# Moving two passes of a weight conversion from VectorE to GpSimd, with the first group's feed-forward blocks made for 128 tokens

## The chip, the cores and the metric

The kernel runs on one core of a Trainium2 chip. The metric is the device time of one execution in microseconds, and it is given as the median over runs. The engines that matter here are TensorE (PE in the profile, with its weight loads as PEld), VectorE (DVE), ScalarE (ACT), GpSimd (POOL) and the queue of SyncE (SP) that issues most transfers.

## The reference: what is computed

Two blocks follow each other. The first is an mLSTM cell over q, k, v of shape (4, 8, 768, 40): batch 4, 8 heads, 768 positions, 40 values per head. The second is a feed-forward block over the 3072 tokens that come out, with 320 features each.

```python
# mLSTM, for each position t:
m_new = max(f + m, i);  C = exp(f + m - m_new) * C + exp(i - m_new) * outer(v, k);  n likewise with k
y[t] = sigmoid(o) * (C @ q) / max(abs(n . q), 1)
# bridge: (B, H, S, D) -> (B*S, H*D), 3072 x 320
a = x @ w1;  b = x @ w2          # 320 -> 1024
out = ((a * b) @ w3) @ w_out     # 1024 -> 1024 -> 320
```

The weights arrive as 64-bit floating-point numbers and are made into 32-bit ones on the chip. The feed-forward block folds w3 and w_out into one matrix of 1024 x 320 before it is used.

## The kernel before, in words

**Steps.** The 3072 tokens are cut into 24 units of 128 tokens (6 chunks of positions by 4 batches). The main loop (L568) runs over steps s; unit s is worked on in step s. A step's work on TensorE is, in this order: the transposes `pt` of k and q (`turn`, L281), the transposes `px` of an earlier unit's output y (`x_trans`, L388), a fold of weights `wp` if one is ready (`w3_mm`), output products `po` (`ffn_out`), up-projections `pa` and `pb` (`up`, L521), their remainder in four 64x64 quarters (`up_rest`, L534), and the cell's small matrix products into the one PSUM tile `cell` (`quarter_work`, L308). The order on TensorE is fixed by a chain of dependencies that `in_order` (L82) adds: each instruction waits in its place.

**Groups.** Four units are a group of 512 tokens, with one `xT` tile. `ups` (L554) lists the up-projections. Each entry is two blocks of 128 hidden features by 256 tokens, for all groups; in group 0 the blocks are ordered so that the first four blocks of features come for both halves of the tokens, then the other four. `n_up` says how many entries a step makes: none up to step 3, one in steps 4 and 5, two from step 6 on. In a step with one entry, `x_trans` of unit s - 2 is placed between `up` and `up_rest` (L595); other steps turn unit s - 3 at their start (L587).

**After the cell's products** VectorE multiplies the scores with the decay weights (`pw`, L346), updates the state (with a product `decayed` on GpSimd between), and makes y of unit s - 1 in `outputs` (L362 to L382). The next step's `cell` products need the same PSUM tile, so they wait for the last reading of it (L370). GpSimd then copies the last 64 features of y once more beside themselves (`twice`, L386), and `x_trans` reads that copy too. `twice(s - 2)` is called in step s ahead of the feed-forward work, on the y that step s - 1 made.

**GpSimd's other work** in a step: two masks of the next unit's weights (`weights`, L278), the weighted values `vw` (`weighted`, L300) and the product of the state with its decay (`decayed`, L305). In the kernel before, `weighted(s)` and, from step 4 on, the first `decayed` of unit s are called at the start of step s.

**Conversion.** `fetch` (L199) brings a piece of a weight as pairs of 32-bit words, `raw`; ScalarE scales the high words (`scale`, L173), and `to_f32` (L175) makes five VectorE passes over the piece: L184, L185 and L186 make the main part `ex` and the power `ma` from the high words, L187 multiplies the low words by that power, L188 adds both. The pieces are, in order, w1 and w2 (10 of 512 columns), w_out (8 of 320) and w3 (16 of 512, of which each is turned by a VectorE transpose, L237). `n_cvt` (L563) says how many pieces are converted at the end of a step: 2, 1, 1, 1, 2, 2, 3, 3, 3, then 2 in each of seven steps. Four rotating `raw` tiles let `fetch` run up to three pieces ahead, on SP's queue.

**Order.** Up to the end of step 6 (`pinned = 7`, L629) the order in which the program calls the instructions is kept on every engine (`keep_order`, L455). After that a planner with its own costs orders the engines other than TensorE.

Of the kernel before, what the change touches and what calls it, by code (L numbers as in the profile page):

```python
# [8 lines left out]
FP = mybir.dt.float32  # L9
U32 = mybir.dt.uint32  # L10
AF = mybir.ActivationFunctionType
OP = mybir.AluOpType
# [4 lines left out]
def kernel(  # L17
# [26 lines left out]
    nc = tc.nc  # L44

    B, H, S, D = q.shape
    L = 64
    P = 128
    NT = S // L
    NT2 = S // P  # L50
    NU = NT2 * B
# [6 lines left out]
    FO = DFF // P  # L58
    KF = DM // P
    REM = DM - KF * P  # L60
    GT = B
# [4 lines left out]
    wst = ctx.enter_context(tc.tile_pool(name="wst", bufs=2))  # L66
# [39 lines left out]
    state = [[const.tile([P, NP, D1], FP, name=f"state{b}_{i}") for i in range(3)] for b in range(B)]  # L106
# [13 lines left out]
    def load(n):  # L120
        for dst, src in ((kbuf[n % NB][:, :, 0:D], k), (qbuf[n % NBQ][:, :, 0:D], q), (vbuf[n % NB][:, :, 0:D], v)):
            if src is not q or n < N_DVE:
                nc.sync.dma_start(out=dst, in_=rows(src, n))
# [11 lines left out]
    def load_o(n):  # L135
        o_t[n] = io.tile([P, H, D], FP, name="o_in", tag="o_in", bufs=4)
        nc.sync.dma_start(out=o_t[n], in_=rows(o_gate, n))

    def load_u(n):
        c, b = divmod(n, B)  # L140
        src = U_d[2 * c:2 * c + 2, b * H:(b + 1) * H, :].rearrange("x h t -> x (h t)")
        for x in range(2):
            nc.sync.dma_start(out=weights_tile(n)[halves[x]].rearrange("p h t -> p (h t)"),
                              in_=src[x:x + 1].to_broadcast([L, H * L]))
# [12 lines left out]
    CW = 512  # L157
# [14 lines left out]
        hi = raw[:, :, 1].bitcast(FP)  # L172
        nc.scalar.mul(out=hi, in_=hi, mul=2.0 ** -111)  # L173

    def to_f32(dst, raw):  # L175

        n = dst.shape[-1]
        lo, hi = raw[:, :, 0], raw[:, :, 1]  # L180
        t = wst.tile([128, n], U32, name="ex", tag="ex", bufs=1)
        r = wst.tile([128, n], U32, name="ma", tag="ma", bufs=1)
        V = nc.vector
        V.tensor_scalar(out=t, in0=hi, scalar1=3, scalar2=None, op0=OP.logical_shift_left)  # L184
        V.scalar_tensor_tensor(out=t, in0=hi, scalar=0x80000000, in1=t, op0=OP.bitwise_and, op1=OP.bitwise_or)  # L185
        V.tensor_scalar(out=r, in0=t, scalar1=0xFF800000, scalar2=None, op0=OP.bitwise_and)  # L186
        V.scalar_tensor_tensor(out=r.bitcast(FP), in0=lo, scalar=2.0 ** -52, in1=r.bitcast(FP), op0=OP.mult, op1=OP.mult)  # L187
        V.tensor_tensor(out=dst, in0=t.bitcast(FP), in1=r.bitcast(FP), op=OP.add)  # L188

    def cols(c0, n):  # L190
# [28 lines left out]
    w3T_t = {}  # L219
    turned_w3, ready_w3 = [], []  # L220

    def scale_next():
        scaled.append(pend.pop(0))
        scale(scaled[-1][1])

    def convert():
        if not scaled:
            scale_next()
        dst, raw, ko, half = scaled.pop(0)
        if dst is not None:  # L230
            to_f32(dst, raw)
            return
        w3 = wst.tile([128, CW], FP, name="w3", tag="w3")
        to_f32(w3, raw)
        if half == 0:
            w3T_t[ko] = wst.tile([128, FO, 128], FP, name="w3T", tag="w3T")
        nc.vector.transpose(out=w3T_t[ko].rearrange("c k (m r) -> c m k r", r=32)[:, 2 * half:2 * half + 2],  # L237
                            in_=w3.rearrange("r (m k c) -> r m k c", m=2, k=FO))
        if half:
            turned_w3.append(ko)  # L240

    def fold():
# [15 lines left out]
    def out_gate(n):  # L258
        nc.scalar.activation(out=o_t[n], in_=o_t[n], func=AF.Tanh, scale=0.5)
# [11 lines left out]
    def weights(n):  # L271
        c, b = divmod(n, B)
        src = weights_tile(n) if c else spread(n)
        pw = weights_tile(n)
        for h in range(H):
            nc.scalar.activation(out=pw[:, h, :], in_=src[:, h, :], func=AF.Exp, bias=aT[:, c, b * H + h:b * H + h + 1])  # L276
        for r in halves:
            nc.gpsimd.affine_select(out=pw[r], in_=pw[r], compare_op=OP.is_ge, fill=0.0, base=0,  # L278
                                    pattern=[[0, H], [1, L]], channel_multiplier=-1)
# [17 lines left out]
    def weighted(n):  # L297
        c, b = divmod(n, B)
        vw_t[n] = sb.tile([P, H, D1], FP, name="vw", tag="vw")
        nc.gpsimd.tensor_tensor(out=vw_t[n], in0=vbuf[n % NB], op=OP.mult,  # L300
                                in1=wT[:, c, b * H:(b + 1) * H].unsqueeze(2).to_broadcast([P, H, D1]))

    def decayed(new, old, n, x):
        c, b = divmod(n, B)
        nc.gpsimd.tensor_tensor(out=new, in0=old, op=OP.mult, in1=decay[:, b * NP:(b + 1) * NP, 2 * c + x:2 * c + x + 1]  # L305
                                .to_broadcast([P, NP, D1]))
# [78 lines left out]
    def twice(n):  # L385
        nc.gpsimd.tensor_copy(out=y_t[n][:, DM:DM + REM], in_=y_t[n][:, KF * P:DM])  # L386

    def x_trans(n):  # L388
        gr, j = divmod(n, GT)
        if j == 0:  # L390
            x_t[gr] = ffn.tile([128, KF + 1, TG], FP, name="xT", tag="xT")
        y = y_t.pop(n)
        px = mps([128, KF + 1, P], "px")
        for cc in range(KF + 1):
            transpose(px[:, cc, :], y[:, cc * P:(cc + 1) * P])
        nc.scalar.copy(out=x_t[gr][:, :, j * P:(j + 1) * P], in_=px)  # L396
# [7 lines left out]
    gates = const.tile([P, 2 * TB], FP, name="gates")  # L404
# [61 lines left out]
    V = nc.vector  # L466
# [7 lines left out]
    for i, r in enumerate(third):  # L474
        V.tensor_tensor_scan(out=M[r, 1:GC + 1], data0=F3[r, :, L - 1], data1=U3[r, :, L - 1], initial=M[r, 0:1],
                             op0=OP.add, op1=OP.max)
# [25 lines left out]
    for i, r in enumerate(third):  # L502
        nc.gpsimd.tensor_tensor(out=pick[r, :, i, :], in0=pair[r].to_broadcast([BH, B * NP, GC]), op=OP.mult,
                        in1=dec[r].unsqueeze(1).to_broadcast([BH, B * NP, GC]))
# [39 lines left out]
    def ffn_out(gr, j):  # L544
        po = mps([P, DM], "po")
        for f in range(FO):
# [4 lines left out]
        nc.scalar.dma_start(out=out[t0:t0 + P, :], in_=o_sb)  # L551


    ups = [(0, [f, f + 1], slice(j * 2 * P, (j + 1) * 2 * P)) for part in range(0, FO, FO // 2) for j in range(2)  # L554
           for f in range(part, part + FO // 2, 2)]
    ups += [(gr, [f, f + 1], slice(j * 2 * P, (j + 1) * 2 * P)) for gr in range(1, NG) for j in range(2)
            for f in range(0, FO, 2)]
    downs = [(gr, j) for gr in range(NG) for j in range(GT)]
    n_up = [0] * 4 + [1] * 2 + [2] * 23 + [0]
    n_down = [0] * 17 + [2] * 10 + [0, 0, 4]  # L560
    w12 = [("w12", i, part) for part in range(2) for i in range(2 * KF + 1)]
    todo = w12[KF * 2 + 1:] + [("wo", i, 0) for i in range(FO)] + [("w3", ko, part) for ko in range(FO) for part in range(2)]
    n_cvt = [2, 1, 1, 1, 2, 2, 3, 3, 3] + [2] * 7  # L563
    pinned = 7
    behind = ExitStack()
    turned, converted, fetched = 0, 2, 2 * KF + 1

    for s in range(len(n_up)):  # L568
        if B <= s + 3 < NU:
            load_u(s + 3)  # L570
        if s + 2 < NU:
            load(s + 2)
            load_o(s + 2)
        if 0 < s < B - 1:
            weights(s + 1)
            out_gate(s)
        if s < NU:
            weighted(s)
            if s >= B:
                decayed(state[s % B][1], state[s % B][0], s, 0)  # L580
            if 0 < s < N_DVE:
                turn(s)
        if 0 <= s - 2 < NU:
            twice(s - 2)
        if N_DVE <= s + 1 < NU:
            load_turned(s + 1)
        while turned < min(s - 2, NU):  # L587
            x_trans(turned)
            turned += 1
        fold()  # L590
        for _ in range(n_down[s]):
            ffn_out(*downs.pop(0))
        now = [ups.pop(0) for _ in range(n_up[s])]
        open_ups = [up(*x) for x in now]
        if len(now) == 1 and turned == s - 2 < NU:  # L595
            x_trans(turned)
            turned += 1

        def rest():
            for x in open_ups:  # L600
                up_rest(*x)

        gated = None
        if s <= NU:
            gated = quarter_work(s, rest)
        else:
            rest()
        with tc.issue_after(gated.ins) if gated else nullcontext():
            if N_DVE <= s + 1 < NU:
                turn(s + 1)  # L610
        if s == 0:
            gate_cols(g, gT, nc.scalar.copy)
            out_gate(0)
            scale_next()
            weights(1)
        if s == NU:
            cell_psum.close()
            banks.append(ctx.enter_context(tc.tile_pool(name="ps_x", bufs=4, space=bass.MemoryType.PSUM)))
        if B - 1 <= s < NU:
            if s + 1 < NU:  # L620
                weights(s + 1)
            out_gate(s)
        for _ in range(n_cvt[s] if s < len(n_cvt) else 0):
            convert()
            converted += 1
        while todo and fetched < converted + (2 if s < 2 else 3):
            fetch(*todo.pop(0))
            fetched += 1
        if s + 1 == pinned:  # L629
            for ins in keep_order(front):  # L630
                behind.enter_context(tc.issue_after(ins))
# [30 lines left out]
```

## Time and profile before

| | us |
|---|---|
| median of 3 runs (lowest, highest) | 483.41 (482.39, 483.81) |
| the profiled execution's own time | 483.81 |
| its span, first to last instruction | 482.1 |
| TensorE busy | 454.6 (94%) |
| VectorE busy | 259.9 (54%) |
| ScalarE busy | 146.8 (30%) |
| GpSimd busy | 86.6 (18%) |

The busy shares are averages over a start, in which VectorE is full and TensorE has gaps, and a long second part, in which TensorE has none. Steps are best told by their last product of the scores (`cell<-qT,kT`), which ends a step on TensorE: at 46.0 us for step 3, 56.5 for step 4, 66.2 for step 5, 78.6 for step 6, 92.7 for step 7 and 109.9 for step 8. From step 8 on TensorE's products follow each other closely to the end.

### The profile page before, as it was taken

To read this page: it belongs to the slowest core of one execution; us is meant where nothing else is said; L and a number is where in the kernel's file an instruction comes from. 1 tells how busy PE (TensorE), PEld (TensorE's weight loads), DVE (VectorE), ACT (ScalarE), POOL (GpSimd) and SP (SyncE) were. 2 spreads that over 40 slices of the span, in tenths; PEclk is the share of its full clock that TensorE was granted. 3 is DMA by queue.
4 is the path that set the end of the run, shared out by engine and by line. 5 is a ranking of instruction groups with operands and counts; after the bars stand their busy time and mean duration, and the time that the engine had idled before them with its cause. 6 is when DMAs were issued, how large, how long until landed. Compare 5 with 4: busy or idle time off the path is not lost.

```text
span 482.1 us, 12855 instructions
## 1 busy us (share of the span) xinstructions
PE 454.6 (94%) x5402; PEld 365.6 (76%) x5402; DVE 259.9 (54%) x526; ACT 146.8 (30%) x399; POOL 86.6 (18%) x165
## 2 busy tenths in 40 slices
PE   3868999799999999999999999999999998999997
PEld 2757877678878888788878787787877877778864
DVE  7797798989886968887451533614325033011110
ACT  3644545443442353354331321311101111011011
POOL 5442322520220322213220211201000000000000
PEclk9995999989999999999999999999999999999999
DMA  8999977599698656433350623324020000000001
GB/s 183 166 166 200 194 139 137 114 203 191 125 189 135 127 127 148 94 66 57 77 132 15 141 57 96 66 81 110 3 82 16 14 27 3 29 14 16 1 14 41
DMA packets 116185, 45.72 MB, mean 95 GB/s; under 512 B 96736, under 2 KB 107168, under 8 KB 116128
## 3 DMA queue, kind: packets, MB, share of 16 engines
q1 hardware_dynamic: 112528, 40.88, 43.4%
q10 hardware_dynamic: 3600, 4.03, 2.4%
q8 instruction: 42, 0.69, 0.6%
q14 instruction: 15, 0.12, 0.1%
HBM read 40.86 MB, written 4.03 MB: 93 GB/s over the span
## 4 chain that ended last, share of the span: by engine, by line
PE 81%; issue 7%; DVE 7%; POOL 2%; DMA 1%; ACT 1%; ACTq 0%; SPq 0%; POOLq 0%; DVEq 0%
PE pa L90 23%; PE po L90 22%; PE pb L90 16%; PE cell L90 9%; PE wp L90 7%; PE pt L93 2%; DVE h L370 1%; PE px L93 1%; PE ub L90 1%; POOL pw L278 1%; DVE o_in L380 1%; DVE h L366 1%; DMA raw<-in_moe_w_out_dram 1%; POOL state L305 1%; DMA gates<-in_i_gate_dram 1%
## 5 line engine op out<-in xcount | busy, mean ns | idle before, releaser
L542 DVE TENSOR_TENSOR ab<-pb,a_sb 128x512 f32<-128x512 f32 x48 | 33.0, 689 | 162.1 <-ACT a_sb L541 162.0
L90 PE MATMUL po<-w3o,ab 128*128 128x320 f32 x384 | 105.4, 433 | 1.3 <-DVE h L370 1.3
L90 PEld LDWEIGHTS po<-w3o,ab 128*128 128x128 f32 x384 | 72.2, 190 | 30.7 <-issue 1.5
L90 PE MATMUL pa<-xT,w 128*128 128x256 f32 x384 | 92.5, 384 | 0.9 <-ACT xT L396 0.6
L90 PE MATMUL pb<-xT,w 128*128 128x256 f32 x384 | 90.8, 379 | 0.0
L90 PEld LDWEIGHTS pa<-xT,w 128*128 128x128 f32 x384 | 73.3, 193 | 14.1 <-ACT xT L396 1.0
L90 PEld LDWEIGHTS pb<-xT,w 128*128 128x128 f32 x384 | 72.9, 190 | 10.3 <-DVE ab L542 0.4
L541 ACT ACTIVATE a_sb<-pa 128x512 f32<-128x512 f32 x48 | 28.6, 595 | 151.3 <-PE pb L90 151.3
L90 PE MATMUL pa<-xT,wr 64*64 64x256 f32 x384 | 47.0, 383 | 0.0
L90 PE MATMUL pb<-xT,wr 64*64 64x256 f32 x384 | 47.0, 383 | 0.0
L305 POOL TENSOR_TENSOR state<-state,decay 128x164 f32<-128x164 f32 x40 | 19.6, 495 | 146.9 <-PE cell L90 91.5
L278 POOL TENSOR_SCALAR_AFFINE_SELECT pw<-pw 64x512 f32<-64x512 f32 x48 | 35.5, 740 | 47.8 <-ACT pw L276 46.2
L276 ACT ACTIVATE pw<-pw,aT 128x64 f32<-128x64 f32 x160 | 40.7, 338 | 8.1 <-DMA pw<-U_d 8.1
L90 PEld LDWEIGHTS pa<-xT,wr 64*64 64x64 f32 x384 | 25.8, 133 | 16.8 <-issue 7.8
L90 PE MATMUL wp<-wo,w3T 128*128 128x320 f32 x128 | 35.9, 433 | 0.1
L90 PEld LDWEIGHTS cell<-vbuf,pw 64*64 64x64 f32 x768 | 27.5, 141 | 6.1 <-issue 1.9
L549 ACT COPY o_sb<-po 128x320 f32<-128x320 f32 x24 | 10.2, 423 | 67.9 <-PE po L90 63.6
L90 PEld LDWEIGHTS wp<-wo,w3T 128*128 128x128 f32 x128 | 23.7, 190 | 9.1 <-PE px L93 0.3
L90 PE MATMUL cell<-vbuf,pw 64*64 64x41 f32 x768 | 27.4, 231 | 2.2 <-issue 1.3
L386 POOL COPY y<-y 128x64 f32<-128x64 f32 x24 | 7.1, 296 | 108.1 <-DVE y L382 104.2
L90 PEld LDWEIGHTS pb<-xT,wr 64*64 64x64 f32 x384 | 25.8, 133 | 0.0
L346 DVE TENSOR_TENSOR pw<-cell,pw 128x512 f32<-128x512 f32 x24 | 16.4, 684 | 15.3 <-PE cell L90 15.2
(89 smaller groups left out, 514.0 us busy)
## 6 DMA issues: line engine op xcount, KB each, us to landing
raw<-in_moe_w_dram SPq DMA_DIRECT2D x64, 128.0 KB, 3.2
pw<-U_d SPq DMA_DIRECT2D x40, 128.0 KB, 3.6
kbuf<-in_k_dram SPq DMA_DIRECT2D x24, 160.0 KB, 4.4
vbuf<-in_v_dram SPq DMA_DIRECT2D x24, 160.0 KB, 5.0
o_in<-in_o_gate_dram SPq DMA_DIRECT2D x24, 160.0 KB, 4.0
out_dram<-o_sb ACTq DMA_DIRECT2D x24, 160.0 KB, 1.9
raw<-in_moe_w_dram SPq DMA_DIRECT2D x7, 512.0 KB, 5.9
qbuf<-in_q_dram SPq DMA_DIRECT2D x17, 160.0 KB, 4.8
```

What stands on the lines that cost most here:

```text
L90: in_order(nc.tensor.matmul(out, lhsT=lhsT, rhs=rhs, start=start, stop=stop))
L93: in_order(nc.tensor.transpose(out, in_, ident[0:n, 0:n]))
L276: nc.scalar.activation(out=pw[:, h, :], in_=src[:, h, :], func=AF.Exp, bias=aT[:, c, b * H + h:b * H + h + 1])
L278: nc.gpsimd.affine_select(out=pw[r], in_=pw[r], compare_op=OP.is_ge, fill=0.0, base=0, pattern=[[0, H], [1, L]], channel_multiplier=-1)
L305: nc.gpsimd.tensor_tensor(out=new, in0=old, op=OP.mult, in1=decay[:, b * NP:(b + 1) * NP, 2 * c + x:2 * c + x + 1] .to_broadcast([P, NP, D1]))
L346: first_read = nc.vector.tensor_tensor(out=pv, in0=ss, in1=pv, op=OP.mult)
L366: nc.vector.tensor_tensor(out=h.rearrange("p (n two) d -> p two n d", two=2), in0=pi, in1=gT[:, c, hs].rearrange("p (n two) -> p two n", t ...
L370: nc.vector.tensor_tensor(out=h[r], in0=ph[x], in1=h[r], op=OP.add)
L386: nc.gpsimd.tensor_copy(out=y_t[n][:, DM:DM + REM], in_=y_t[n][:, KF * P:DM])
L541: nc.scalar.mul(out=a_sb, in_=pa, mul=UP ** -2)
L542: nc.vector.tensor_tensor(out=ab_t[gr][j][:, fs[0]:fs[-1] + 1, t0:t0 + a_sb.shape[-1]], in0=pb, in1=a_sb, op=OP.mult)
L549: nc.scalar.copy(out=o_sb, in_=po)
```

## The change

The last two passes of a conversion (the product with the low words and the sum) run on GpSimd for the last two pieces of each step from step 4 to step 14, 22 pieces in all. GpSimd's product takes no scalar, so ScalarE first multiplies the low words by 2^-52, in place. The two scratch tiles of such a piece lie in `gates`, a buffer that is free then; there is one pair of them, as there is one pair of `ex` and `ma`. The transposes of w3 pieces that GpSimd made are called at the end of the next step. `weighted` and the first `decayed` of unit s + 1 are called at the end of step s from step 4 on, ahead of the conversions. Group 0's up-projections are made for four blocks of features by 128 tokens, from step 3 on: one entry in steps 3 to 6, then two.

```diff
-    def to_f32(dst, raw):
+    def to_f32(dst, raw, E=None):
         n = dst.shape[-1]
         lo, hi = raw[:, :, 0], raw[:, :, 1]
-        t = wst.tile([128, n], U32, name="ex", tag="ex", bufs=1)
-        r = wst.tile([128, n], U32, name="ma", tag="ma", bufs=1)
+        if E is None:
+            t = wst.tile([128, n], U32, name="ex", tag="ex", bufs=1)
+            r = wst.tile([128, n], U32, name="ma", tag="ma", bufs=1)
+        else:
+            t, r = (gates[:, i * CW:i * CW + n].bitcast(U32) for i in range(2))
...
-        V.scalar_tensor_tensor(out=r.bitcast(FP), in0=lo, scalar=2.0 ** -52, in1=r.bitcast(FP), op0=OP.mult, op1=OP.mult)
+        if E is None:
+            V.scalar_tensor_tensor(out=r.bitcast(FP), in0=lo, scalar=2.0 ** -52, in1=r.bitcast(FP), op0=OP.mult, op1=OP.mult)
+        else:
+            V = E
+            nc.scalar.mul(out=lo.bitcast(FP), in_=lo, mul=2.0 ** -52)
+            V.tensor_tensor(out=r.bitcast(FP), in0=lo.bitcast(FP), in1=r.bitcast(FP), op=OP.mult)
         V.tensor_tensor(out=dst, in0=t.bitcast(FP), in1=r.bitcast(FP), op=OP.add)
...
-    def convert():
+    def convert(E=None):
...
-        to_f32(w3, raw)
-        if half == 0:
+        to_f32(w3, raw, E)
+        if ko not in w3T_t:
             w3T_t[ko] = wst.tile([128, FO, 128], FP, name="w3T", tag="w3T")
+        if E is None:
+            turn_w3(w3, ko, half)
+        else:
+            unturned.append((w3, ko, half))
+    unturned, halves_in = [], {}
+    def turn_w3(w3, ko, half):
         nc.vector.transpose(out=w3T_t[ko].rearrange("c k (m r) -> c m k r", r=32)[:, 2 * half:2 * half + 2],
                             in_=w3.rearrange("r (m k c) -> r m k c", m=2, k=FO))
-        if half:
+        halves_in[ko] = halves_in.get(ko, 0) + 1
+        if halves_in[ko] == 2:
             turned_w3.append(ko)
...
-    ups = [(0, [f, f + 1], slice(j * 2 * P, (j + 1) * 2 * P)) for part in range(0, FO, FO // 2) for j in range(2)
-           for f in range(part, part + FO // 2, 2)]
+    ups = [(0, list(range(f, f + 4)), slice(j * P, (j + 1) * P)) for f in (0, 4) for j in range(GT)]
...
-    n_up = [0] * 4 + [1] * 2 + [2] * 23 + [0]
+    n_up = [0] * 3 + [1] * 4 + [2] * 22 + [0]
...
-    pinned = 7
+    pinned, early = 7, 4
...
+    def weigh(n):
+        weighted(n)
+        if n >= B:
+            decayed(state[n % B][1], state[n % B][0], n, 0)
...
         if s < NU:
-            weighted(s)
-            if s >= B:
-                decayed(state[s % B][1], state[s % B][0], s, 0)
+            if s <= early:
+                weigh(s)
...
-        for _ in range(n_cvt[s] if s < len(n_cvt) else 0):
-            convert()
+        if early <= s < NU - 1:
+            weigh(s + 1)
+        while unturned:
+            turn_w3(*unturned.pop(0))
+        for i in range(n_cvt[s] if s < len(n_cvt) else 0):
+            convert(nc.gpsimd if i + 2 >= n_cvt[s] and early <= s < len(n_cvt) - 1 else None)
             converted += 1
```

More of the change, by code (lines that the diff above doesn't have):

```diff
@@ L230, in convert @@
         if dst is not None:
-            to_f32(dst, raw)
+            to_f32(dst, raw, E)
             return
         w3 = wst.tile([128, CW], FP, name="w3", tag="w3")
-        to_f32(w3, raw)
-        if half == 0:
+        to_f32(w3, raw, E)
+        if ko not in w3T_t:
             w3T_t[ko] = wst.tile([128, FO, 128], FP, name="w3T", tag="w3T")
+        if E is None:
[4 more added lines that the diff above has]
+    def turn_w3(w3, ko, half):
         nc.vector.transpose(out=w3T_t[ko].rearrange("c k (m r) -> c m k r", r=32)[:, 2 * half:2 * half + 2],
                             in_=w3.rearrange("r (m k c) -> r m k c", m=2, k=FO))
-        if half:
+        halves_in[ko] = halves_in.get(ko, 0) + 1
+        if halves_in[ko] == 2:
             turned_w3.append(ko)
```

## The prediction

> **What bounds the kernel now.** I read the page's engine shares and slices first, then the busy times cut at the ends of the steps, then each engine's instructions in order of time.
>
> ```profile
> PE 454.6 (94%) x5402; PEld 365.6 (76%) x5402; DVE 259.9 (54%) x526; ACT 146.8 (30%) x399; POOL 86.6 (18%) x165
> PE   3868999799999999999999999999999998999997
> DVE  7797798989886968887451533614325033011110
> PEclk9995999989999999999999999999999999999999
> ```
>
> TensorE has no gap worth the name after the ninth slice (12 us each). Before it there are gaps, VectorE is nearly full, and the granted clock falls to half for a while. Only in this start can a change of VectorE's work be worth anything. The next lines are steps 5 to 8 and then step 9 (window, then TensorE, weight loads, VectorE, ScalarE, GpSimd busy with counts, clock, transfers):
>
> ```profile
> 56.40:66.10 9.70, 8.54 (x178) 7.15 (x172) 8.39 (x18) 5.47 (x17) 3.18 (x6) 1.00 0.94 154
> 66.10:78.50 12.40, 12.39 (x203) 10.35 (x201) 11.14 (x25) 5.34 (x17) 3.25 (x6) 1.00 0.74 138
> 78.50:92.60 14.10, 12.97 (x210) 10.91 (x204) 12.87 (x25) 9.25 (x30) 9.18 (x14) 1.00 0.67 120
> 92.60:109.90 17.30, 14.42 (x207) 11.80 (x204) 15.25 (x38) 6.39 (x17) 3.31 (x6) 0.90 0.97 186
> 109.90:122.40 12.50, 12.50 (x206) 10.81 (x205) 11.61 (x28) 5.71 (x16) 0.77 (x3) 1.00 0.94 192
> ```
>
> Step 9 is full at 12.5 us. Steps 7 and 8 do the same TensorE work with 1.1 and 2.9 us idle. TensorE's own lines say why (start, duration, in brackets the idle time and who ended it):
>
> ```profile
> 62.15 0.67 PE L93 MATMUL px<-ident,y 128*128 128x128 f32 x3 [1.17 <-DVE y L382]
> ...
> 80.23 0.66 PE L93 MATMUL pt<-ident,qbuf 128*128 128x128 f32 x4 [1.07 <-DVE ab L542]
> ...
> 95.82 0.66 PE L93 MATMUL pt<-ident,qbuf 128*128 128x128 f32 x4 [2.57 <-DVE ab L542]
> ...
> 97.18 3.38 PE L90 MATMUL pa<-xT,w 128*128 128x256 f32 x8 [0.30 <-DVE ab L542]
> 100.39 1.89 PE L90 MATMUL pb<-xT,w 128*128 128x256 f32 x8
> ```
>
> The `ab` products are late because three conversions stand ahead of them on VectorE. The 3.38 us are the same 8 instructions as the 1.73 that the next group leaves: the clock was at half after the 2.57 us gap, for 3.3 us. So VectorE's conversions cost step 5 1.2, step 7 1.1 and step 8 some 4.5 us. That, with the idle time of steps 2 to 4, is all there is to win. GpSimd in step 5:
>
> ```profile
> 59.53 0.74 POOL L300 TENSOR_TENSOR vw<-vbuf,wT 128x328 f32<-128x328 f32 x1
> 60.22 0.46 POOL L305 TENSOR_TENSOR state<-state,decay 128x164 f32<-128x164 f32 x1
> 62.14 0.30 POOL L386 COPY y<-y 128x64 f32<-128x64 f32 x1 [1.45 <-DVE y L382]
> ```
>
> GpSimd now waits for y (62.00) and copies its tail at once; `px` follows at 62.15. In the change this copy, `twice(s - 2)`, is called behind the conversions of step s - 1, and in the steps whose order is kept it cannot pass them.
>
> **Prices.** A VectorE conversion of 512 columns takes 3.15 us (61.92 to 65.07). Its first three passes, which stay, take 1.62 with their gaps; for 320 columns 1.25 of 2.3. GpSimd's products: 164 columns 0.46, 328 columns 0.74, so 1.7 ns a column and 0.19 fixed; 512 columns come to 1.04 and 320 to 0.73, a pair to 2.1 and 1.5 with 0.1 for the hand-over 2.2 and 1.6. Ends for a 512-column pass: 0.69, the mask's mean less contention (1.37 for two, one input), and 1.68, from the 96x256 product in the start, 0.84 with VectorE busy beside it. I take the middle price, of the same operation undisturbed, since VectorE stands still during most of these passes.
>
> [...]
>
> A 128-column up-projection is not in the trace. Below: half of a 256-column one, 0.108 (1.73 for 8). Above: 0.128, a transpose of 128 columns (8 in 1.02). I take 0.128, the same width. An entry of 32 is then 4.1 us instead of 3.46, its 32 quarters 1.0 instead of 0.9. ScalarE's 22 scalings of the low words (0.63 each, 14 us) lie in its idle time (4 to 7 us in each of these steps); VectorE's and ScalarE's `ab` work keeps its shape and number. Uncovered, ScalarE's two scalings would hold the copies of k and q by 1.3 us, ahead of a wait that is longer.
>
> **Part 1, earlier up-projections (steps 3 and 4).** In step 3 the first entry starts when xT is copied, at 40.3. The clock is at half there (0.50 from 36 to 48). By the 97.18 row it comes back about 3.3 us after dense work begins, so I give 0.6 for it: up to 45.0, `px` 0.5, quarters 1.0, cell 2.45 (107.44 to 109.9): step 3 ends at 48.9 against 46.0. From there y takes 5.45 (56.5 to 62.0), `twice` 0.45. Step 4: `pt` 1.0, up to 54.0, `px` waits for the copy until 54.7, then 0.5 + 1.0 + 2.45: 58.65 against 56.5. y at 64.1.
>
> **Part 2, conversions on GpSimd (steps 5 and 6).** Both pieces use the same two scratch slices, so VectorE's first pass of piece B waits until GpSimd's sum of piece A has read them. The chain after y is 1.6 + 2.2 + 1.6 + 2.2 + 0.45 for `twice` = 8.0 us, where VectorE alone needed 6.2 and `twice` needed none of it. `px` of step 5 thus comes at 72.1. It stands ahead of the quarters and the cell's products. TensorE has its up-projections done at 63.8 and idles 8.3 us, far more than the 2.57 that brought the half clock above. So `px` 0.85 (as at 47.70, half clock), quarters 1.9, cell 2.7: step 5 ends at 77.6, against 66.2; y at 83.0, against 74.1. Step 5's pieces are 512 and 320 columns: 1.6 + 2.2 + 1.25 + 1.6 + 0.45 = 7.1, `px` of step 6 at 90.1, and the same 5.45: step 6 ends at 95.6 against 78.6. It made one entry where before it made two.
>
> **Part 3, steps 7 and 8.** No `px` comes between there, and step 8 turns a y one step older, so GpSimd's queue is covered. `pt` 1.0, two entries 8.2, quarters 2.0, cell 2.45: 13.65, to 109.2 (92.7 before). VectorE's passes for w_out, 1.25 us instead of 2.3, and the wait between them end at 107.5, as `ab` becomes ready. Step 8 with `px` 0.5: 14.15, to 123.4 (109.9 before): +13.4. The stalls of 1.1 and 4.5 us are gone in this; the narrower products take back 0.7 to 0.8 for each of four entries.
>
> **Part 4, the rest.** From step 9 TensorE is full, and has the same products. The folds come one step later, from step 11, with two in step 17: nothing, since step 17's output products waited for the last fold before too. `raw` is released by GpSimd's product instead of VectorE's, within 0.4 us of it, and SP's queue of fetches and loads is no later in steps that are longer. `weighted` one step ahead is covered: GpSimd then has 5 us until the cell asks. A step's VectorE chain with the waits (5.45 + 7.6 + 1.4 of `ab` + 1.4 of transposes = 15.9) fits the 16.8 us of a step with a fold (137.17 to 155.01 is one, 17.8), not the 12.5 of steps 9 and 10, which now have none. Between 0 and 3 each; I take 0, as `ab` can go between the passes there.
>
> **Sum.** +2.9, -0.8, +9.3, +5.6, -0.5, -3.1 by step, +13.4. Against the profiled execution's 483.8 that is 497.2; the median is 0.4 lower, so 497 us.
>
> [...]
>
> **Rivals.** *The copy is not held up* (13 in 100): the real order lets `twice` go ahead. Then `px` of step 5 comes at 64.6, the cell ends at 68.5, VectorE is ready at 70.2 (8.0 less the last pair, plus `ab`), y 75.7; step 6 likewise ends at 80.1, 7 at 93.7, 8 at 107.9: -2.1, 481.3, faster. There `px` waits 0.8 and 2.5 us; the sign turns when each wait is 1 us longer. Against it: up to step 6 every engine's lines follow the program's order. *The later steps suffer too* (12): GpSimd's passes stand ahead of `decayed`, or steps 9 and 10 become VectorE's: 3.3 each on top, 504. *Cheap GpSimd* (10): passes of 0.69, 0.108 a product and no clock loss give step ends 48.0, 57.7, 73.4, 88.3, 100.4, 113.0: +3.1, 486.5. *As worked out* (65): by its middle bounds 490 to 503. With passes of 1.68 and half clock through all the quarters and the cell's products (7.75 us from `px` on instead of 5.45) it is +24, 508. The range is 486 to 508.
>
> No change within 0.3% (1.5 us, about what a measurement of this kernel can tell from none) is only likely between the first rival and the third: 0.04. Faster 0.1, slower 0.86.
>
> **What the profile after would show.** Right: in steps 5 and 6 `px` with 6 to 10 us idle before it, ended by GpSimd's copy of y; four GpSimd products between y and that copy, 1.0 us each at 512 columns; VectorE waiting 2 us for GpSimd ahead of a second L184; clock 0.5 after it; steps 7 and 8 without idle time at 13.7 and 14.2 us. Wrong: if `px` waits for VectorE's y as now; if the passes are below 0.7 or above 1.5; or if time is lost after step 9.

## The result, and the profile after

The changed kernel takes 512.1 us (median of four, 509.07 to 513.54), the kernel before 483.6: a ratio of 1.058, 95% interval 1.052 to 1.064. Here and below a median is that of all executions, and the ratios leave out three executions in a slower state (one of run 3, one of run 9, one of the kernel before beside runs 9 and 10). The prediction, 497 us, had the direction right and put the loss at less than half of what it is. The profiled execution took 509.07 us with a span of 507.4, 25.3 us more than the span of 482.1 before. The readings below explain these 25.3 us. The median lies 3.0 us above the profiled run; the granted clock over whole executions went from 0.953 to 0.963, and no run here says why.

The end of each step on TensorE, its last product of the scores, carries the whole comparison:

| step | 3 | 4 | 5 | 6 | 7 | 8 | 9 | 10 | 11 | 14 | 16 | 17 | end |
|---|---|---|---|---|---|---|---|---|---|---|---|---|---|
| before | 46.0 | 56.5 | 66.2 | 78.6 | 92.7 | 109.9 | 122.4 | 139.5 | 157.3 | 207.6 | 241.2 | 265.7 | 482.1 |
| after | 48.6 | 60.1 | 79.8 | 99.7 | 113.2 | 128.2 | 142.5 | 158.8 | 175.5 | 228.4 | 261.9 | 290.7 | 507.4 |
| difference | 2.6 | 3.6 | 13.6 | 21.1 | 20.5 | 18.2 | 20.1 | 19.3 | 18.2 | 20.7 | 20.7 | 25.0 | 25.3 |
| predicted | 2.9 | 2.1 | 11.4 | 17.0 | 16.5 | 13.4 | 13.4 | 13.4 | 13.4 | 13.4 | 13.4 | 13.4 | 13.4 |

So 3.6 us are lost in steps 3 and 4, 17.5 in steps 5 and 6, 2.9 come back in steps 7 and 8, and then 2.5 are lost over steps 9 to 14 and 4.3 in step 17. First the profile of the changed kernel, engine shares and slices:

```profile
PE 460.1 (91%) x5658; PEld 375.7 (74%) x5658; DVE 237.2 (47%) x482; ACT 158.4 (31%) x421; POOL 135.4 (27%) x209
PE   3769826698889999999999999999999999899997
DVE  7886735277966755567942145153152340210110
PEclk9797969599989999999999999999999999999999
```

VectorE has 23 us less work and GpSimd 49 us more. TensorE has a hole in the sixth to eighth slices (2, 6 and 6 tenths busy, where it had 9, 9 and 7), and the granted clock is reduced in the sixth and the eighth (0.6 and 0.5). The busy times of steps 4 to 10, cut at their ends (window, then TensorE, weight loads, VectorE, ScalarE, GpSimd, clock, transfers):

```profile
48.63:60.09 11.46, 9.10 (x205) 8.30 (x205) 8.08 (x17) 6.71 (x19) 3.19 (x6) 1.00 0.95 161
60.09:79.80 19.71, 10.33 (x204) 9.64 (x205) 8.25 (x18) 5.29 (x16) 8.16 (x10) 0.74 0.64 115
79.80:99.68 19.88, 11.65 (x205) 10.91 (x205) 7.85 (x18) 7.53 (x21) 7.35 (x10) 0.71 0.45 81
99.68:113.20 13.52, 13.52 (x265) 13.33 (x266) 10.31 (x25) 8.83 (x28) 6.01 (x9) 0.91 0.22 58
113.20:128.17 14.97, 13.21 (x268) 12.55 (x269) 12.08 (x24) 7.54 (x19) 12.65 (x20) 1.00 0.88 186
128.17:142.48 14.31, 12.94 (x204) 10.78 (x205) 11.79 (x24) 6.15 (x16) 5.72 (x7) 1.00 0.79 170
142.48:158.75 16.27, 14.37 (x205) 11.94 (x205) 10.53 (x23) 6.64 (x14) 7.98 (x10) 0.90 0.63 124
```

In steps 5 and 6 no engine is busy for more than 60% of the time: everything waits in turn. TensorE's lines say for what (start, duration, idle time before and who ended it):

```profile
65.69 0.41 PE L93 MATMUL px<-ident,y 128*128 128x128 f32 x2 [1.01 <-DVE y L400]
74.47 0.47 PE L93 MATMUL px<-ident,y 128*128 128x128 f32 x1 [8.38 <-POOL y L404]
...
85.39 0.41 PE L93 MATMUL px<-ident,y 128*128 128x128 f32 x2 [0.99 <-DVE y L400]
93.03 0.48 PE L93 MATMUL px<-ident,y 128*128 128x128 f32 x1 [7.24 <-POOL y L404]
```

Two of the three transposes go as soon as VectorE has y. Only the third reads the part that GpSimd copies, and it stands idle for 8.38 and 7.24 us. GpSimd in step 5, in order:

```profile
67.20 1.29 POOL L195 TENSOR_TENSOR gates<-raw,gates 128x512 f32<-128x512 f32 x1 [2.97 <-issue]
68.56 1.26 POOL L196 TENSOR_TENSOR w<-gates 128x512 f32<-128x512 f32 x1
71.61 1.29 POOL L195 TENSOR_TENSOR gates<-raw,gates 128x512 f32<-128x512 f32 x1 [1.78 <-issue]
72.97 1.26 POOL L196 TENSOR_TENSOR w<-gates 128x512 f32<-128x512 f32 x1
74.18 0.24 POOL L404 COPY y<-y 128x64 f32<-128x64 f32 x1
```

The copy of 0.24 us stands behind two conversions. VectorE in the same stretch shows the shared scratch, whose first pass waits for GpSimd's sum:

```profile
66.64 0.43 DVE L189 TENSOR_SCALAR gates<-gates 128x512 uint32<-128x512 uint32 x1
69.86 0.43 DVE L187 TENSOR_SCALAR gates<-raw 128x512 uint32<-128x512 uint32 x1 [2.79 <-POOL w L196]
...
77.54 0.69 DVE L560 TENSOR_TENSOR ab<-pb,a_sb 128x512 f32<-128x512 f32 x1 [6.07 <-ACT a_sb L559]
```

After step 8 the waits are of another kind. In step 10 a transpose of a w3 piece waits for GpSimd on VectorE's queue, `ab` stands behind it, and TensorE's `pt` behind `ab`:

```profile
143.48 0.71 DVE L254 STREAM_TRANSPOSE w3T<-w 128x512 f32<-128x512 f32 x1 [2.82 <-POOL w L196]
144.22 1.29 DVE L560 TENSOR_TENSOR ab<-pb,a_sb 128x512 f32<-128x512 f32 x2
```

```profile
144.97 0.66 PE L93 MATMUL pt<-ident,qbuf 128*128 128x128 f32 x4 [1.90 <-DVE ab L560]
...
262.23 8.78 PE L90 MATMUL wp<-wo,w3T 128*128 128x320 f32 x32
```

The second of these lines is step 17, with two folds in a row: 32 products where each fold takes 16 and 4.3 us. Step 10 has no fold any more, but with the waits on VectorE it still took 16.3 us, against 17.1 with its fold before. Of these 16.3 us, 1.9 are the wait and some 1.4 the lower clock behind it (the row of step 10 above: 14.37 us busy at 0.90 for as many products as step 9 does in 12.94). So one fold's time was not saved where it left and was paid where it arrived.

### The profile page after: what moved, and what is told of

It reads as the page before. It is cut to its first block, busy times and chain, and to the rows that moved or that the text cites. A ratio compares the mean times of both kernels' runs of the same rounds, so it can differ in the third digit from the quotient of the medians.

```text
span 507.4 us, 13428 instructions
## 1 busy us (share of the span) xinstructions
PE 460.1 (91%) x5658; PEld 375.7 (74%) x5658; DVE 237.2 (47%) x482; ACT 158.4 (31%) x421; POOL 135.4 (27%) x209
## 4 chain that ended last, share of the span: by engine, by line
PE 68%; POOL 5%; issue 5%; DVE 4%; DMA 2%; ACT 1%; SPq 1%; POOLq 0%; DVEq 0%; ACTq 0%
PE po L90 20%; PE pa L90 19%; PE pb L90 13%; PE cell L90 7%; PE wp L90 6%; POOL gates L195 2%; PE pt L93 2%; PE px L93 1%; DMA raw<-in_moe_w_out_dram 1%; DMA qbuf<-in_q_dram 1%; ACT pw L294 1%; POOL w L196 1%; SPq L168 1%; POOL pw L296 1%; DVE h L388 1%
## 5 line engine op out<-in xcount | busy, mean ns | idle before, releaser
L90 PE MATMUL pa<-xT,w 128*128 128x256 f32 (+1 forms) x448 | 94.9, 360 | 2.3 <-DVE ab L560 1.8
L90 PE MATMUL pb<-xT,w 128*128 128x256 f32 (+1 forms) x448 | 92.8, 353 | 0.2 <-issue 0.2
L90 PEld LDWEIGHTS pa<-xT,w 128*128 128x128 f32 x448 | 78.0, 198 | 14.0 <-DVE ab L560 2.3
L90 PEld LDWEIGHTS pb<-xT,w 128*128 128x128 f32 x448 | 77.3, 195 | 8.5
L90 PE MATMUL pa<-xT,wr 64*64 64x256 f32 (+1 forms) x448 | 49.1, 362 | 0.0
L90 PE MATMUL pb<-xT,wr 64*64 64x256 f32 (+1 forms) x448 | 49.1, 362 | 0.0
L90 PEld LDWEIGHTS pa<-xT,wr 64*64 64x64 f32 x448 | 29.9, 139 | 15.1 <-issue 7.2
L195 POOL TENSOR_TENSOR gates<-raw,gates 128x512 f32<-128x512 f32 (+1 forms) x22 | 26.6, 1209 | 52.8 <-DVE gates L189 17.6
L93 PE MATMUL px<-ident,y 128*128 128x128 f32 x72 | 13.9, 295 | 18.3 <-POOL y L404 15.6
L90 PEld LDWEIGHTS pb<-xT,wr 64*64 64x64 f32 x448 | 29.9, 139 | 0.0
```

Of the source, the lines that this page charges most:

```text
L90: in_order(nc.tensor.matmul(out, lhsT=lhsT, rhs=rhs, start=start, stop=stop))
L93: in_order(nc.tensor.transpose(out, in_, ident[0:n, 0:n]))
L195: V.tensor_tensor(out=r.bitcast(FP), in0=lo.bitcast(FP), in1=r.bitcast(FP), op=OP.mult)
```

## The experiments

The ratios are to the kernel before on the same chip, which ran there at 484.6 to 486.0 us in the median. All step ends are from the profiled executions.

**1. The earlier, narrower up-projections alone.**

```diff
 kernel before
+    ups = [(0, list(range(f, f + 4)), slice(j * P, (j + 1) * P)) for f in (0, 4) for j in range(GT)]
+    n_up = [0] * 3 + [1] * 4 + [2] * 22 + [0]
```

> The kernel before with the earlier, 128-token up-projections of group 0 alone; all conversions stay on VectorE. Theory (most of the loss is TensorE waiting for GpSimd's copy of y behind the conversions): 484 to 488 us, no idle time over 1.5 us before px. Rival 1 (the narrower, earlier products and the clock they meet cost the time): 495 us or more. Rival 2 (the conversions slow VectorE by contention): like the theory here.

Measured: 491.8 us, 1.012 (1.006 to 1.017). Between the two; that no idle time over 1.5 us would stand before `px` was wrong. The profiled span is 8.1 us longer. Steps 3 and 4 end 2.7 and 4.1 us later, as in the change, step 6 6.8 us later. Its three longest waits from step 4 on:

```profile
59.67 0.25 PE L90 MATMUL cell<-vw,kbuf 64*64 64x41 f32 x2 [1.81 <-issue]
78.33 0.87 PE L93 MATMUL px<-ident,y 128*128 128x128 f32 x3 [3.30 <-DVE y L382]
130.57 6.24 PE L90 MATMUL wp<-wo,w3T 128*128 128x320 f32 x16 [3.62 <-DVE w3T L237]
```

A step with one entry turns the y of the step just past, and has only 3.6 us of products to lay before it, so step 6 waits for y where the kernel before turned none. And the first fold, in step 10, waits for its w3 piece. This part costs some 6 us of its own by the medians (8 by the profiled executions), though it is not where the change lost most.

**2. GpSimd's passes alone**, with the 256-token products.

```diff
 changed kernel
-    ups = [(0, list(range(f, f + 4)), slice(j * P, (j + 1) * P)) for f in (0, 4) for j in range(GT)]
-    n_up = [0] * 3 + [1] * 4 + [2] * 22 + [0]
+    (both as in the kernel before)
```

> The changed kernel with the 256-token up-projections of the kernel before; the conversions stay on GpSimd. Theory: only one px is held up in the steps with the program's order (step 5; the next comes two steps after its y), so about half of the wait: 495 to 500 us. Rival 1 (narrow products): back to 484 to 488. Rival 2 (contention): as the change, 508 to 513.

Measured: 500.7 us, 1.032 (1.026 to 1.039). As the theory said, there is one held transpose (8.37 us idle before it, ended by GpSimd's copy, in step 5) and none in step 6. With the first run: 1.2% and 3.2% apart, 5.8% together. The parts add to less than the whole; the second held transpose, of step 6, is in the profile only where both are there.

**3. The copy of y first.**

```diff
 changed kernel
-        if 0 <= s - 2 < NU:
+        if 0 <= s - 2 < early - 1:
             twice(s - 2)
...
         if early <= s < NU - 1:
             weigh(s + 1)
+        if early <= s <= NU:
+            twice(s - 1)
```

> The changed kernel with GpSimd's copy of y called at the end of the step that makes it, ahead of that step's conversions. Theory: the waits of 8.4 and 7.2 us before px go, and with them the half clock: 490 to 495 us, what is left being the later steps (some 7 us) and VectorE. Rival 1 and rival 2: 508 to 513, less at most 3.

Measured: 498.1 us, 1.025 (1.018 to 1.032); 3 us above the range expected, and far from the rivals. Steps 5 to 8 now end at 69.8, 85.1, 97.5 and 110.2 us: step 8 is 0.3 us behind the kernel before instead of 18.2. Moving a copy of 0.24 us on its queue took back nearly all that was lost up to there:

```profile
65.73 0.67 PE L93 MATMUL px<-ident,y 128*128 128x128 f32 x3 [1.00 <-DVE y L400]
78.77 0.87 PE L93 MATMUL px<-ident,y 128*128 128x128 f32 x3 [4.40 <-DVE y L400]
...
163.90 1.11 PE L93 MATMUL pt<-ident,qbuf 128*128 128x128 f32 x4 [3.81 <-DVE ab L560]
```

The 4.40 us in step 6 are the wait for y that run 1 had there (3.30). The 3.81 us in step 12 are the largest wait after step 8. Its cause is VectorE's transpose at 161.38, which had waited 2.81 us for GpSimd's sum, with two `ab` behind it. Nearly all of the 13.4 us by which this span is longer come after step 8: 6.7 in step 12 (23.5 us instead of 16.8, at a mean clock of 0.85) and 4.4 in step 17. So of the 17.9 us won back up to step 8 only 11.9 are left at the end: behind step 8 this run loses 13.1 us, the change lost 7.1.

**4. GpSimd's passes from step 7 on.**

```diff
-            convert(nc.gpsimd if i + 2 >= n_cvt[s] and early <= s < len(n_cvt) - 1 else None)
+            convert(nc.gpsimd if i + 2 >= n_cvt[s] and 7 <= s < len(n_cvt) - 1 else None)
```

> The changed kernel with GpSimd's passes from step 7 on, where the program's order is no longer kept. Theory: no held px; the later steps' loss of some 7 us stays: 490 to 495 us. Rival 1: 505 to 513. Rival 2 (contention over all steps): 500 to 508, as 8 of 11 steps keep it.

Measured: 497.7 us, 1.024 (1.019 to 1.030), the same as with the copy first, and 2.7 above the range. Step 12 has the same wait of 3.81 us. In the whole, keeping the pieces out of the steps with a fixed order helps as much as moving the copy, though step 8 ends 5.5 us behind the kernel before, and not 0.3.

**5. Copy first, and GpSimd's passes in steps 4 to 7 only**, so that w3 stays on VectorE.

```diff
 as 3
-    ... early <= s < len(n_cvt) - 1 ...
+    ... early <= s < 8 ...
```

> Copy first, and GpSimd's passes only in steps 4 to 7, so that the w3 pieces stay on VectorE and are turned at once. Theory (what copy-first leaves, 13 us after step 8, comes from VectorE waiting for GpSimd's sums ahead of the ab products, and from a fold that leaves step 10 for step 17): step 17 has one fold again, no VectorE wait for a GpSimd sum after step 8, 482 to 489 us. Rival (the loss after step 8 comes from the planner's order with the narrow products, as in the run of them alone): 492 to 498.

Measured: 492.6 us, 1.016 (1.010 to 1.022). The theory's time was missed and the rival's met. Step 17 has one fold again, and no wait for a GpSimd sum is left there, but step 10's fold waits 3.94 us for w3T, and its 16 products then take 6.10 us, against 4.54 in the kernel before. That is the wait that the narrow products had alone (3.62 us in run 1). The fold is not reached early (at 126.2 us, against 123.8 in the kernel before); the w3 piece is late. In the kernel before VectorE converts the first w3 piece between the passes that make y, from 114.54 us on; in runs 1 and 5 it does so only behind them, from 120.1 and 120.6 us on.

**6. A second pair of scratch tiles**, with the copy first: `ex` and `ma` for the last but one piece, `gates` for the last.

```diff
 as 3
-        if E is None:
+        if own:
             t = wst.tile([128, n], U32, name="ex", tag="ex", bufs=1)
...
+            convert(..., own = i + 1 < n_cvt[s] or not early <= s < len(n_cvt) - 1)
```

> Copy first, with a second pair of scratch tiles: the last but one piece of a step uses ex and ma, the last one the slices of gates. Theory: VectorE's wait of 2.8 us ahead of the second piece goes in every step up to 14; the transposes still wait for GpSimd and the fold stays in step 17: 490 to 495 us. Rival (the shared scratch is the main cause after step 8): 483 to 489. Rival (scratch is not waited for at a place that counts): 496 to 499.

Measured: 494.9 us, 1.021 (1.015 to 1.027), at the upper end of the theory's range. VectorE no longer waits ahead of the second piece; but its passes then run while GpSimd works, and L188 and L189 take 1.67 and 1.39 us where they took 0.69 and 0.43. The 3.8 us of step 12 remain.

**7 and 8. The 256-token products, copy first, steps 4 to 7, with one and with two pairs of scratch.**

```diff
 as 5 (run 8: with the two pairs of 6)
-    ups = [(0, list(range(f, f + 4)), slice(j * P, (j + 1) * P)) for f in (0, 4) for j in range(GT)]
-    n_up = [0] * 3 + [1] * 4 + [2] * 22 + [0]
+    (both as in the kernel before)
```

> As the run with copy first and GpSimd's passes in steps 4 to 7 only, with the 256-token up-projections of the kernel before. Theory: px of step 6 no longer waits for y (4.4 us with one entry there); the stalls of VectorE in steps 5 to 8 of the kernel before (some 6.8 us) shrink: 478 to 484 us. Rival (moving passes gains nothing, as VectorE waits as long as it saved): 484 to 490.

> The same with two pairs of scratch tiles. Theory: VectorE is free 2.2 to 2.8 us earlier in steps 4 to 7: 476 to 483 us, no slower than with one pair. Rival: 484 to 490.

Measured: 486.9 us, 1.005 (1.002 to 1.009), and 485.2 us, 1.0015 (0.9988 to 1.0042). Both theories were too hopeful. With two pairs step 8 ends 2.6 us ahead of the kernel before, and step 10 0.7 behind it: the fold waits 1.57 us for w3T, and `pt` and `pa` wait 1.4 us for `ab` in step 9. The lead is gone before it counts.

**9 and 10. One piece of each step on GpSimd**, the first, beside VectorE's five passes of the second, and w3 turned in the same step; in steps 4 to 15, and in 4 to 7 only.

```diff
 as 8
+        for i in range(n_cvt[s] if s < len(n_cvt) else 0):
+            convert(nc.gpsimd if i == 0 and 4 <= s < 16 else None, not (i == 0 and 4 <= s < 16))
+            converted += 1
         while unturned:
             turn_w3(*unturned.pop(0))
```

> 256-token products, copy first, and GpSimd's two passes for the first piece of a step only (steps 4 to 15), with scratch of its own; the second piece is VectorE's, so that GpSimd's 2.6 us lie beside 3.1 us of VectorE's passes, and both w3 halves are turned at the end of the same step. Theory (the loss was in waiting for GpSimd, not in the moving): no VectorE wait for a GpSimd sum over 0.5 us, the fold stays in steps 10 to 17, step 8 ends 1 to 3 us before that of the kernel before: 479 to 484 us. Rival (moving passes costs by contention or by later w3 pieces whatever the order): 485 to 490.

> The same in steps 4 to 7 only. Theory: as the run before up to step 8, then VectorE's w3 conversions are the limit of the first fold in step 10 (it waited 1.6 us for w3T where step 8 came early): 482 to 486 us, slower than with one piece in all steps. Rival: no different from it.

Measured: 487.1 us, 1.003 (0.999 to 1.008), and 486.1 us, 1.003 (1.000 to 1.006). No gain, and no difference between them: the rivals hold. The twelve executions of run 9 lie in two groups, 482.9 to 485.4 and 488.9 to 491.3 us, and the profiled one (483.5) is of the lower. Up to step 9 VectorE nowhere waits for a GpSimd sum. From step 10 on run 9 has six such waits of 1.5 to 3.1 us, against its theory (the third line below is the first of them), but TensorE waits for none of them; run 10 has no such wait and is no faster. VectorE, then GpSimd, in the run with one piece in all steps:

```profile
75.30 1.49 DVE L188 SCALAR_TENSOR_TENSOR ex<-raw,ex 128x320 uint32<-128x320 uint32 x1
76.83 1.28 DVE L189 TENSOR_SCALAR ma<-ex 128x320 uint32<-128x320 uint32 x1
...
132.99 0.71 DVE L254 STREAM_TRANSPOSE w3T<-w 128x512 f32<-128x512 f32 x1 [2.81 <-POOL w L196]
```

```profile
75.15 1.30 POOL L195 TENSOR_TENSOR gates<-raw,gates 128x512 f32<-128x512 f32 x1 [1.23 <-DMA raw<-in_moe_w_out_dram]
76.52 1.40 POOL L196 TENSOR_TENSOR wr<-gates 128x512 f32<-128x512 f32 x1
```

The same two VectorE passes take 0.49 and 0.33 us when GpSimd is idle. Moving two passes of 512 columns saves VectorE about 1.5 us and, where GpSimd's 2.7 us lie beside other passes of this kind, costs it 1.95. GpSimd loses less by it: 0.15 us here (1.30 and 1.40 against 1.29 and 1.26), 0.4 us in step 5 (1.36 and 1.60). From the first pass after y to the next `ab`, VectorE took 6.25 and 5.44 us in steps 5 and 6 of the kernel before, and 6.55 and 5.79 in run 9, which has two passes less there. In run 8, with both pieces on GpSimd, it took 5.11 and 4.72. So with two pieces VectorE did come to `ab` sooner, and with one it did not.

**11. GpSimd's passes in steps 4 to 7 only, with nothing else altered** (the copy stays behind them).

> The changed kernel with GpSimd's passes in steps 4 to 7 only; the copy of y stays behind them. Theory: the two waits before px stay (7 to 9 us each, step 8 ends 18 us later than before), the fold goes back from step 17 to step 10, and steps 9 and 10 no longer wait for GpSimd's sums, so the 6.8 us lost after step 8 go: 503 to 506 us. Rival (the loss after step 8 belongs to the order after the held steps): 509 to 513.

Measured: 505.5 us, 1.043 (1.038 to 1.049), as the theory said. The two waits are there unchanged, 8.37 and 7.24 us, and step 8 ends 18.1 us late; from there to the end it loses 2.6 us more, where the change lost 7.1. So the w3 pieces on GpSimd cost 4.5 us of the profiled 25.3 (by the ratios of all executions some 7). Of the 2.6 us that are left, 1.8 are in step 9, which takes 14.3 us in both runs.

**12. The kernel before with the program's order kept up to step 8.**

```diff
-    pinned = 7
+    pinned = 9
```

> The kernel before with the program's order kept up to step 8 instead of 6. Question: whether the stalls of steps 7 and 8 (3.9 us and a half clock of 1.7) come from GpSimd's masks and state products, which the planner sets beside the conversions of step 6, where VectorE's passes take up to twice as long (0.33 to 0.77). Theory (contention): 480 to 483 us. Rival (the three conversions ahead of ab are the limit in any order): 484 to 489.

Measured: 489.8 us, 1.010 (1.005 to 1.016), slower than either expected. But it answers the question. In the kernel before the planner sets GpSimd's masks of two units beside the three w_out conversions of step 6, which take 8.96 us (86.09 to 95.04); here GpSimd has only the copy of y beside them, and they take 7.0. The kernel before, then this run:

```profile
85.78 1.62 POOL L278 TENSOR_SCALAR_AFFINE_SELECT pw<-pw 64x512 f32<-64x512 f32 x2
...
86.09 0.77 DVE L184 TENSOR_SCALAR ex<-raw 128x320 uint32<-128x320 uint32 x1
```

```profile
87.84 0.32 DVE L184 TENSOR_SCALAR ex<-raw 128x320 uint32<-128x320 uint32 x1
...
94.32 0.49 DVE L188 TENSOR_TENSOR wo<-ex,ma 128x320 f32<-128x320 f32 x1
```

Steps 7 and 8 together take 27.2 us instead of 31.4, and the 2.57 us that `pt` waited for `ab` in step 8 are 0.50. The gain is then lost in steps 9 and 10, where `pt` waits 4.51 us for `ab` and the 16 products of the fold behind it take 5.78 us, against 4.54 in the kernel before. Whether an order can be found that keeps the 4.2 us was not tried.

## Why the prediction was right or wrong

Of the 15 us between 497 and 512.1, 4.1 were lost in excess of the sum up to step 6, 0.7 in steps 7 and 8, and 7.1 behind step 8, where the sum has nothing; the rest is that the median lies 3.0 us above the profiled execution, where 0.4 below was taken. Without the 7.1 us the time would lie inside the stated range.

**Part 2, the held transposes: right, and shown.** The mechanism, its place in steps 5 and 6, the chain through the shared scratch and the half clock after the gaps (0.50 granted) are all in the profile, and runs 2, 3, 4 and 11 each remove or keep the waits as the theory says. Up to step 6 the loss was 21.1 us, predicted 17.0. The terms that were too small:

- A GpSimd pass of 512 columns was put at 1.04 us, by the products with a broadcast operand. It took 1.27 (1.29 and 1.26), one of 320 columns 0.87 instead of 0.73. From the end of y to the start of the copy there were 8.6 us in step 5, predicted 7.6.
- Step 4 lost 1.54 us in a gap of TensorE that no engine ended ("issue"), which was not in the sum. At this place, the cell's products of step 4, it came in every run with narrow products, 0.8 to 2.4 us, and in none with wide ones. Its cause was not examined.
- After the second gap the clock stayed at half (0.50) until 102.0 us, so that `px`, the quarters and the cell took 6.65 us, not 5.45.

**Part 1, the earlier products: right within 1.5 us for steps 3 and 4**, and too dear in the price of a product: 16 of 128 columns follow each other in 1.79 us, 0.112 each, near the lower end of the two bounds and not at the 0.128 that was taken. What it missed is run 1: in step 6 there is a `px` where there was none, with too little work ahead of it. In the change that wait was inside the longer one.

**Part 3, steps 7 and 8: nearly right.** They took 13.5 and 15.0 us for 13.65 and 14.15. In step 8 `pt` and `pa` still waited for `ab` (0.89 and 0.87 us), which was said to be gone; the cheaper products took back about half of it. The reading of the kernel before on which this rested, that `ab` is late there because three conversions stand ahead of it, holds only in part: in run 12 the same three stand ahead of it in step 8, unslowed, and `pt` waits 0.50 us instead of 2.57.

**Part 4 is the step that failed.** It read "Between 0 and 3 each; I take 0, as `ab` can go between the passes there", and of the folds "nothing". The profile has 7.1 us after step 8. `ab` did not go between the passes: it stood behind a w3 transpose that had waited 2.8 to 2.9 us for GpSimd, in step 10 and again in steps 12 and 13, and TensorE then waited 1.90, 0.68 and 0.62 us for `ab`. A fold that moves to a later step is free only if the step that it leaves becomes shorter by as much. Steps 9 and 10 were recognised as too short for VectorE's chain of 15.9 us, and step 10 took 16.3; the sum should have charged the fold's 4.3 us to step 17 for that reason. Run 11 puts the two together at 4.5 of the 7.1; step 9 lost 1.8 of the rest, with or without w3 on GpSimd, and its cause was not tested. This was the second rival's mechanism, that steps 9 and 10 become VectorE's, at 12 in 100 and 6.6 us; it was no alternative to the main case but the end of it. That its size came close is partly luck, as it holds no second fold in step 17.

**The cheap and the first rival fell** with the lines of steps 5 and 6. Run 3 is the first rival's condition, a copy that is not held up: step 8 ended 2.3 us later than the rival had it (110.2 for 107.9), and the kernel was slower, not 2.1 us faster. With wide products its lead came about (run 8, 2.6 us at step 8) and was lost again by step 10.

## What to carry to other kernels

Before work is put on another engine, list everything that stands behind it on that engine's queue, and look for the smallest instruction that a full engine waits for: here a 0.24 us copy behind 7 to 9 us of conversions cost some 18 us by step 8, and calling it first took them back there (18.2 us behind became 0.3). At the end only 11.9 us of this were left, as the later steps lost more than in the change. Work that is moved to a second engine helps only if the first does not wait for its results, or for its scratch, ahead of something urgent. And a piece of work that changes step is free only where the step that it leaves was bounded by that engine.

## What the runs showed of the hardware that was not expected

VectorE's conversion passes over SBUF (on-chip memory) took up to 3.9 times as long beside the two products of GpSimd's conversion: 1.49 us instead of 0.49 for a pass with a second tensor, and 1.28 instead of 0.33 for one with a constant (run 9); 1.67 instead of 0.69 and 1.39 instead of 0.43 in run 6. GpSimd's own two went from 1.29 and 1.26 us to 1.36 and 1.60 (run 9, step 5), so VectorE paid most of the price. Beside the masks a pass with a constant took 0.77 us instead of 0.33 (the kernel before, step 6). The `h` passes, which read PSUM, where TensorE's products land, kept their time there: 0.49 us for the first and 1.01 for the two others beside the masks (from 82.42 us in the kernel before), and the same with GpSimd idle (from 112.98 us).

In the gap of 8.4 us before `px` the granted clock went from 1.00 (up to 67 us) to 0.50, and it stayed there for 3.6 us after work began again (74.5 to 78.0); after the second gap, of 7.2 us, it was at 0.50 for 9.0 us (93.0 to 102.0). No run here shows why the second lasted longer.
